# A soft mixture of experts behind sliding-window attention: the expert sum in two PSUM banks, seven filling matmuls, and the output in eleven tiles

## The chip, the cores and the metric

The kernel runs on one core of a Trainium2 chip. The metric is the time of one execution on the device in microseconds (us), inputs and output in the chip's HBM. The core has five engines, which run side by side and wait for each other by semaphores: TensorE (PE; its weight loads are listed apart as PEld), VectorE (DVE), ScalarE (ACT), GpSimd (POOL) and SyncE (SP). Sixteen DMA engines move data between HBM and SBUF, the memory beside the engines. TensorE writes into PSUM, eight banks of 512 fp32 columns on 128 partitions, and DVE and ACT read from there.

## What is computed

The first part is attention over 8 batches, 8 heads, 576 tokens of 64 values. Each token sees 32 earlier ones, side by side for heads 0 to 3 and every fourth for heads 4 to 7. Its result x (4608 rows of 512) goes through a soft mixture of 8 experts with 4 slots each:

```python
logits = x @ phi                                  # 4608 x 32
d = exp(logits - logits.max(0)); d /= d.sum(0)    # each slot over all rows
slot_input = (d.T @ x).reshape(8, 4, 512)
for e in range(8):
    h = np.maximum(slot_input[e] @ w1[e], 0.0)    # 4 x 1024
    slot_out[e] = h @ w2[e]                       # 4 x 512
c = exp(logits - logits.max(1)); c /= c.sum(1)    # each row over the slots
out = c @ slot_out.reshape(32, 512)               # 4608 x 512, fp32
```

## The kernel before

The kernel is written with a tile framework, which puts the instructions in order on each engine, finds the semaphore waits and may move an instruction ahead where nothing holds it back. Only GpSimd's order is as written. GpSimd issues all big loads: q, k and v of the eight batches, and the weights, which are cast from fp32 to fp16 on the way. Each batch and later each expert has one of eight homes in SBUF, so that the weights of expert e can be loaded when batch e is done.

Attention takes most of the time. `unit` goes through four head pairs of each batch, and the front of the expert part is worked into the same loop. `front_logits` (line 430) writes ET, the exponentials of the logits, with 32 slots on 128 partitions (each slot stands four times) and one column for each of the 4608 rows. `front_rows` (line 460) multiplies blocks of 128 columns of ET by `quarter` (0.25), which gives the sum over the slots for 128 rows, and writes the reciprocals to `rrow`, one column for each block of 128 rows.

The expert part starts when the inputs of the slots, siT, are ready. `expert_in` (line 662) does two experts: 32 matmuls with w1 (line 667), a Relu on ACT (line 675), four transposes (line 678) and two copies by DVE into hTp (line 683). `expert_out` (line 688) does eight matmuls of 512 columns with w2. Each takes 32 columns of the array, four of them side by side, and all add into one bank `sop`: 32 slots on four groups of partitions, whose sum is taken later because ET stands four times. The loop calls them for four pairs; the last lines are `expert_out(6)` and `expert_out(7)`. The w2 of expert 7 comes in two halves (lines 250 and 251), chunks 0 to 3 and 4 to 7. ACT then casts `sop` to `so` in fp16 (line 708).

The output goes in 18 tiles of 256 rows (lines 718 to 741). Each partition of a tile holds two neighbouring rows, so that one partition's piece in HBM is 4 KB. For each of the two, one matmul of 512 columns (line 729) multiplies 128 columns of ET (every second one) by `so`. ACT takes the first and DVE the second out of PSUM, each multiplied by its column of `rrow` (lines 731 and 733), into one of six buffers `ot`. SyncE issues one transfer for each tile (line 739). The first tile is made in halves of 256 columns and issued in two transfers (line 737), one for each of the two rows.

Of the kernel before, what the change touches and what calls it, by code (L numbers as in the profile page):

```python
# [9 lines left out]
FP32 = mybir.dt.float32  # L10
# [7 lines left out]
S = 576  # L18
# [6 lines left out]
N_ROWS = B * S  # L25
DMODEL = H * D
E_EXP = 8
# [7 lines left out]
RD, ND = 12, 48  # L35
CL = S // DIL
DW = CL + 16
NU = 4 * B
NV = 2

# [14 lines left out]
def kernel(  # L55
# [10 lines left out]
    nc = tc.nc  # L66
# [5 lines left out]
    ident = consts.tile([128, 128], FP16, name="ident")  # L72
# [4 lines left out]
        out=q0,  # L77
        in_=q[0, 0:2].rearrange("h s d -> (h s) d").rearrange("(g p r) d -> p g (r d)", g=2, r=RP),
# [7 lines left out]
    def kept(shape, name, dt=FP16):  # L86
        return keep.tile(shape, dt, name=name, tag=name)

    ET = kept([128, N_ROWS + 64], "ET")
    csum = kept([128, 2 * B - 2], "csum", FP32)  # L90
    rrow = kept([128, 2 * N_ROWS // 256], "rrow", FP32)
    quarter = kept([128, 1], "quarter")
# [37 lines left out]
    for i in range(NV):  # L130
        nc.vector.memset(vp[i][:, :, :, D : D + 1], 1.0)

    hTp = [kept([128, 8, 60], f"hTp{e}") for e in range(4)]
# [10 lines left out]
    ring = ctx.enter_context(  # L144
        tc.tile_pool(name="ring", bufs=2, space=bass.MemoryType.PSUM)
    )
# [3 lines left out]
    raws, w_tiles = {}, {}  # L150
# [108 lines left out]
    def transposes(u):  # L259
        b, hp = unit(u)  # L260
        for nm in ("q", "k"):
            if nm == "q":
                dst = qT_pool.tile([128, S], FP16, name=f"qT{u}", tag="qT")
                qTs[u] = dst
            else:
                dst = kTp if hp < 2 else kTd
                kTs[u] = dst
            if hp < 2:
                raw = raws[b][nm + "p"]
                rg = ring.tile([128, RP, NP], FP16, name=f"rg{nm}{u}", tag="ring")  # L270
                for r in range(RP):
                    for h in range(2):
                        nc.tensor.transpose(  # L273
                            rg[64 * h : 64 * h + 64, r, :],
                            raw[:, 2 * hp + h, D * r : D * r + D],
                            ident[0:NP, 0:NP],
                        )
                nc.scalar.copy(  # L278
                    out=dst[:, 0:S].rearrange("c (p r) -> c p r", r=RP),
                    in_=rg.rearrange("c r p -> c p r"),  # L280
                )
            else:
                raw = raws[b][nm + "d"]
                rg = ring.tile([128, 3, 4, ND], FP16, name=f"rg{nm}{u}", tag="ring")
                for a in range(3):
                    for cc in range(2):
                        j = 2 * a + cc
                        nc.tensor.transpose(  # L288
                            rg[:, a, 2 * cc : 2 * cc + 2, :].rearrange("c h p -> c (h p)"),
                            raw[:, hp - 2, 128 * j : 128 * j + 128],  # L290
                            ident[0:NP, 0:NP],
                        )
                (nc.scalar.copy if nm == "q" else nc.vector.tensor_copy)(  # L293
                    out=dst[:, 0:S].rearrange("c (g p a) -> c g p a", g=4, a=3),
                    in_=rg.rearrange("c a g p -> c g p a"),
                )

    def scores(u):
# [3 lines left out]
        for part in range(2):  # L302
# [4 lines left out]
            else:  # L307
                todo = [(DW * cc, CL * (2 * cc + part), CL * (2 * cc + part), CL) for cc in range(2)]
                todo += [(DW * cc + CL, None, CL * (2 * cc + part) + 128, 16) for cc in range(2)]
            for at, k0, q0, n in todo:  # L310
                for g in range(2):
                    ks = q0 - 32 * g - 64 * (at // DW) if k0 is None else k0
                    nc.tensor.matmul(  # L313
# [9 lines left out]
    def softmax_parts(u, tiles):  # L323
        b, hp = unit(u)
        for part in range(2):
# [14 lines left out]
            if part == 0:  # L340
                pr = dil_pool.tile([128, 2, 2, 2, DW], FP16, name=f"pd{u}", tag="pd")
            nc.scalar.activation(  # L342
                out=pr[:, part].rearrange("p c e t -> p e c t"),
                in_=st[:, :, 0 : 2 * DW].rearrange("p e (c t) -> p e c t", c=2),
                func=AF.Exp,
                scale=SCALE,
            )
        if hp < 2:
# [10 lines left out]
            out=P2.rearrange("p a c s t -> p (a c) s t")[:, :, :, 0:16],  # L359
            in0=pr[:, :, :, 128:DW].rearrange("p a c (s t) -> p (a c) s t", s=2),  # L360
            in1=mask[:, QW + 64 :].rearrange("p (c s t) -> p c s t", c=8, s=2),
# [90 lines left out]
    def rows(to, tokens, rhs, start, stop):  # L452
        for n, (part, at, step) in enumerate(row_blocks):
            w = step * (part.stop - part.start - 1) + 1
            nc.tensor.matmul(
                to[part, min(n, 9), :], tokens(at, at + w, step), rhs, start=start, stop=stop,
                skip_group_check=True,
            )

    def front_rows(b):  # L460
        r0 = b * S
        t0, t1 = r0 // 256, (r0 + S) // 256
        ep = ring.tile([128, 11, N_SLOTS], FP32, name=f"e{b}", tag="ring")
        if b < B - 1:
            rows(ep, lambda a, z, s: ET[:, r0 + a : r0 + z : s], ident[:, 0:N_SLOTS], True, True)
            nc.vector.tensor_copy(out=Er[b % 2], in_=ep[:, 0:10])
        for n in range(2 * (t1 - t0)):
            c0 = 256 * t0 + 256 * (n // 2) + n % 2
            nc.tensor.matmul(
                ep[:, 10, n : n + 1], ET[:, c0 : c0 + 255 : 2], quarter, start=True, stop=True  # L470
            )
        nc.vector.reciprocal(out=rrow[:, 2 * t0 : 2 * t1], in_=ep[:, 10, 0 : 2 * (t1 - t0)])

    def front_slots(b):
        up = ring.tile([128, DMODEL], FP32, name=f"u{b}", tag="ring")
# [126 lines left out]
    transposes(2)  # L602
    for u in range(NU + 5):
        if u + 1 < NU:
            st = scores(u + 1)
        if u < NU:
            values(u)
        if u + 1 < NU:
            softmax_parts(u + 1, st)
        if u + 3 < NU:  # L610
            transposes(u + 3)
# [11 lines left out]
        if u == 1:  # L623
            spread_phi()
        if u == NU:
            last = ps_s.tile([128, 2, 512], FP32, name="last", tag="s")
# [20 lines left out]
        out=siT,  # L647
# [9 lines left out]
    ps_h = tc.alloc_tile_pool(name="ps_h", bufs=2, space=bass.MemoryType.PSUM)  # L657
    ps_t = tc.alloc_tile_pool(name="ps_t", bufs=2, space=bass.MemoryType.PSUM)
    ps_so = tc.alloc_tile_pool(name="ps_so", bufs=1, space=bass.MemoryType.PSUM)
    sop = ps_so.tile([128, DMODEL], FP32, name="sop", tag="sop")  # L660

    def expert_in(pr):
        hp_ = ps_h.tile([128, 512], FP32, name=f"h{pr}", tag="h")
# [21 lines left out]
                in_=tp[:, :, 2 * ee : 2 * ee + 2, 4 * e : 4 * e + 4].rearrange("p i f s -> p f i s"),  # L685
            )

    def expert_out(e):
        for ch in range(8):
            j = ch % 4  # L690
            nc.tensor.matmul(
                sop[32 * j : 32 * j + 32, :],
                hTp[e % 4][:, ch, 28 - 4 * e : 60 - 4 * e],
                w_tiles[e][1][:, ch, :],
                start=(e == 0 and ch < 4),
                stop=(e == E_EXP - 1 and ch >= 4),
                skip_group_check=True,
            )

    for pr in range(4):  # L700
        expert_in(pr)
# [1 line left out]
            expert_out(2 * pr - 2)  # L703
            expert_out(2 * pr - 1)
    expert_out(6)
    expert_out(7)
    so = keep.tile([128, DMODEL], FP16, name="so", tag="so")
    nc.scalar.copy(out=so, in_=sop)
    ps_so.release()
    ps_t.release()  # L710
    ps_h.release()
# [2 lines left out]

    ps_f = tc.alloc_tile_pool(name="ps_f", bufs=3, space=bass.MemoryType.PSUM)
    out_pool = ctx.enter_context(tc.tile_pool(name="outp", bufs=1))
    ots = [out_pool.tile([128, 2, DMODEL], FP32, name=f"ot{i}", tag=f"out{i}") for i in range(6)]
    for t in range(N_ROWS // 256):
        ot = ots[t % 6]
        rows = out[256 * t : 256 * t + 256, :].rearrange("(m j) d -> m j d", j=2)  # L720
        for j in range(2):
            cols = ET[:, 256 * t + j : 256 * t + j + 255 : 2]
            scale = rrow[:, 2 * t + j : 2 * t + j + 1]
            halves = ((0, 256), (256, 512)) if t == 0 else ((0, 512),)
            for n, (d0, d1) in enumerate(halves):
                n = j if t else n
                fp = ps_f.tile([128, DMODEL], FP32, name=f"f{t}_{j}{n}", tag=f"f{n}")
                fp = fp[:, 0 : d1 - d0]
                nc.tensor.matmul(fp, cols, so[:, d0:d1], start=True, stop=True)  # L729
                if n == 0:  # L730
                    nc.scalar.activation(out=ot[:, j, d0:d1], in_=fp, func=AF.Copy, scale=scale)  # L731
                else:
                    nc.vector.tensor_scalar(  # L733
                        out=ot[:, j, d0:d1], in0=fp, scalar1=scale, scalar2=None, op0=ALU.mult
                    )
            if t == 0:
                nc.sync.dma_start(out=rows[:, j], in_=ot[:, j])
        if t > 0:
            nc.sync.dma_start(
                out=rows.rearrange("m j d -> m (j d)"), in_=ot.rearrange("m j d -> m (j d)")  # L740
            )
    ps_f.release()

# [29 lines left out]
```

## Time and profile before

| what | value |
|---|---|
| median of 3 runs | 185.99 us (185.93 to 188.54) |
| profiled execution | 186.0 us |
| its span, first to last instruction | 184.2 us |
| TensorE busy, DVE busy, ACT busy | 80%, 64%, 63% of the span |
| weights and inputs by GpSimd's queue | 30.79 MB in 22480 packets, 94.4% of the DMA engines' span |
| transfers of SyncE's queue, mostly the output | 9.89 MB in 3376 packets, 13.6% |

The span is counted from the first to the last instruction; what lies before and after it makes the difference to the execution's own time. In the profile's groups, `out<-in` names what an instruction writes and reads, with numbers of buffers left out, and L729 is line 729. A chain of waits is followed back from the last instruction, at each step to what released it. The granted clock is the share of TensorE's full speed that the chip allowed. Ends of matmuls are modelled, so a busy TensorE need not be at its peak.

### The profile page before, as it was taken

What the parts mean: (1) busy time and instruction counts of PE and PEld (TensorE: products, weight loads), DVE (VectorE), ACT (ScalarE), POOL (GpSimd) and SP (SyncE); (2) the same over time, 40 slices, a digit from 0 to 9 for tenths busy, and PEclk for the clock granted to TensorE, in tenths of its full rate; (3) what the DMA queues carried; (4) which work ended last, traced back from release to release, by engine and by line L of the source; (5) the groups of instructions that cost most, each with busy time, mean ns of one, the idle gap of its engine ahead of it and who ended that gap; (6) DMA issues with size and microseconds to landing.
All of it is one profiled execution on the core that took longest, in us unless ns stands there. A gap on an engine that the chain in (4) does not pass through costs nothing.

```text
span 184.2 us, 6078 instructions
## 1 busy us (share of the span) xinstructions
PE 147.0 (80%) x2595; PEld 101.0 (55%) x2595; DVE 117.1 (64%) x363; ACT 116.5 (63%) x208; POOL 48.3 (26%) x77
## 2 busy tenths in 40 slices
PE   1879889699899899979978989989698983895300
PEld 1647666566676667757666667667585330331000
DVE  7605995948778788797786877869801110595610
ACT  2248879677888797798789698878131220785510
POOL 7754545455554545410011010022000000000000
PEclk9999999979999999999999999999965798589755
DMA  5999999999999999999999999999999994399995
GB/s 106 190 202 204 200 202 203 202 201 204 200 203 200 204 201 206 215 211 221 205 223 210 222 206 218 213 216 221 210 222 213 209 212 87 128 422 418 421 418 245
DMA packets 25883, 41.06 MB, mean 223 GB/s; under 512 B 1792, under 2 KB 20352, under 8 KB 24832
## 3 DMA queue, kind: packets, MB, share of 16 engines
q0 software_dynamic: 22480, 30.79, 94.4%
q1 hardware_dynamic: 3376, 9.89, 13.6%
q8 instruction: 20, 0.33, 0.6%
q14 instruction: 7, 0.06, 0.1%
HBM read 62.02 MB, written 9.44 MB: 388 GB/s over the span
## 4 chain that ended last, share of the span: by engine, by line
DMA 54%; PE 15%; issue 14%; ACT 5%; DVE 4%; POOL 4%; ACTq 0%; POOLq 0%
DMA home<-in_moe_w_dram 32%; DMA home<-in_q_dram 6%; DMA home<-in_k_dram 6%; DMA out_dram<-ot 5%; DMA home<-in_v_dram 5%; PE f L729 3%; PE l L434 2%; ACT pd L342 2%; PE sel L203 2%; PE rgx L414 1%; PE o L393 1%; PE rgq L273 1%; POOL home L182 1%; DVE P L351 1%; ACT qT L278 1%
## 5 line engine op out<-in xcount | busy, mean ns | idle before, releaser
L398 DVE TENSOR_TENSOR x<-o,rc 128x384 f16<-128x384 f32 x64 | 30.0, 482 | 0.5
L330 ACT ACTIVATE pr<-s 128x960 f16<-128x960 f32 (+1 forms) x32 | 24.8, 783 | 0.8 <-PE s L313 0.8
L342 ACT ACTIVATE pd<-s 128x640 f16<-128x640 f32 x32 | 21.0, 706 | 0.8 <-PE s L313 0.7
L160 POOL DMA_DIRECT2D home<-in_v_dram x24 | 16.6, 692 | 16.3 <-DMA home<-in_k_dram 9.6
L733 DVE TENSOR_SCALAR ot<-f,rrow 128x512 f32<-128x512 f32 (+1 forms) x19 | 13.3, 720 | 11.1 <-PE f L729 7.3
L203 PE MATMUL sel<-home,pick 32*128 32x256 f16 x128 | 16.8, 291 | 1.2 <-DMA home<-in_v_dram 0.7
L414 PE MATMUL rgx<-ident,x 128*128 128x128 f16 x160 | 14.6, 223 | 3.8 <-ACT qT L293 3.5
L333 DVE TENSOR_TENSOR Pp<-pr,mask 128x960 f16<-128x960 f16 (+2 forms) x48 | 16.4, 394 | 0.3 <-ACT pr L330 0.3
L731 ACT ACTIVATE ot<-f,rrow 128x512 f32<-128x512 f32 (+1 forms) x19 | 12.3, 665 | 6.8 <-DMA out_dram<-ot 4.3
L397 DVE RECIPROCAL rc<-o 128x6 f32<-128x6 f32 x64 | 10.0, 175 | 9.8 <-PE o L393 9.6
L278 ACT COPY qT<-rgq 128x576 f16<-128x576 f16 x16 | 10.3, 642 | 9.3 <-PE rgq L273 8.8
L420 ACT COPY xT<-rgx 128x512 f16<-128x512 f16 x16 | 9.7, 605 | 9.7 <-PE rgx L414 9.7
L729 PE MATMUL f<-so,ET 128*128 128x512 f16 (+1 forms) x38 | 12.3, 454 | 4.4 <-ACT ot L731 3.4
L237 POOL DMA_DIRECT2D home<-in_moe_w_dram x8 | 4.5, 565 | 37.6 <-PE rgq L288 30.1
L211 ACT CAST vp<-sel 128x512 f16<-128x512 f32 x16 | 9.4, 590 | 7.7 <-PE sel L203 7.0
L414 PEld LDWEIGHTS <-x 128*128 128x128 f16 x160 | 9.8, 98 | 7.4 <-issue 5.3
L273 PEld LDWEIGHTS <-home 96*64 96x64 f16 x384 | 11.1, 116 | 4.3 <-issue 2.4
L434 PE MATMUL l<-xT,phi 128*128 128x288 f16 x64 | 11.4, 318 | 2.2 <-ACT qT L278 2.0
L182 POOL DMA_DIRECT2D home<-in_k_dram x16 | 10.6, 662 | 9.4 <-DMA home<-in_q_dram 7.9
L293 DVE COPY kTd<-rgk 128x576 f16<-128x576 f16 x16 | 12.0, 751 | 0.4 <-PE rgk L288 0.4
L393 PE MATMUL o<-vp,Pp 128*128 128x65 f16 x288 | 12.0, 197 | 0.0
L293 ACT COPY qT<-rgq 128x576 f16<-128x576 f16 x16 | 10.4, 647 | 2.2 <-PE rgq L288 1.7
(106 smaller groups left out, 286.6 us busy)
## 6 DMA issues: line engine op xcount, KB each, us to landing
home<-in_moe_w_dram POOLq DMA_DIRECT2D x15, 1024.0 KB, 32.6
out_dram<-ot SPq DMA_DIRECT2D x17, 512.0 KB, 5.0
home<-in_k_dram POOLq DMA_DIRECT2D x16, 288.0 KB, 10.0
home<-in_q_dram POOLq DMA_DIRECT2D x15, 288.0 KB, 9.9
home<-in_v_dram POOLq DMA_DIRECT2D x16, 256.0 KB, 10.0
home<-in_moe_w_dram POOLq DMA_DIRECT2D x2, 512.0 KB, 30.3
home<-in_v_dram POOLq DMA_DIRECT2D x8, 64.0 KB, 8.8
out_dram<-ot SPq DMA_DIRECT2D x2, 256.0 KB, 2.1
```

Source lines behind the costliest of these rows:

```text
L160: nc.gpsimd.dma_start(out=dst, in_=v[b, h0 : h0 + n_h, r0 : r0 + 4 * n_p, :].rearrange("h (p r) d -> p h (r d)", r=4),)
L203: nc.tensor.matmul(sel[:, n, 0], pick[rows, r].rearrange("p i j -> p (i j)"), raw[rows, :, r, :], start=(r == 0), stop=(r == 3), tile_posi ...
L293: (nc.scalar.copy if nm == "q" else nc.vector.tensor_copy)(out=dst[:, 0:S].rearrange("c (g p a) -> c g p a", g=4, a=3), in_=rg.rearrange(" ...
L330: nc.scalar.activation(out=pr, in_=st[:, :, 0:n], func=AF.Exp, scale=SCALE)
L333: nc.vector.tensor_tensor(out=Pp[:, :, b0 : b0 + nb, 0:w], in0=pr[:, :, at : at + nb * w].rearrange("p h (t c) -> p h t c", c=w), in1=mask ...
L342: nc.scalar.activation(out=pr[:, part].rearrange("p c e t -> p e c t"), in_=st[:, :, 0 : 2 * DW].rearrange("p e (c t) -> p e c t", c=2), f ...
L393: nc.tensor.matmul(to, lhs, rhs, start=(n == 0), stop=(n == len(mms) - 1), skip_group_check=True)
L398: nc.vector.tensor_tensor(out=x[:, blocks[0] : blocks[0] + nb, D * hl : D * hl + 2 * D].rearrange("p t (h d) -> p t h d", h=2), in0=ot[:, ...
L414: nc.tensor.transpose(rg[:, 128 * blk : 128 * blk + 128], x[:, blk, hl : hl + 128], ident)
L434: nc.tensor.matmul(lp, phi4[:, kc].rearrange("p a s -> p (a s)"), xT[:, kc, 288 * c : 288 * c + 288], start=(kc == 0), stop=(kc == 3),)
L729: nc.tensor.matmul(fp, cols, so[:, d0:d1], start=True, stop=True)
L733: nc.vector.tensor_scalar(out=ot[:, j, d0:d1], in0=fp, scalar1=scale, scalar2=None, op0=ALU.mult)
```

## The change

Three things change. The expert sum `sop` becomes two banks, of which the first 256 columns of each are used: `expert_out` goes twice over the chunks, with 256 columns of w2 each time, and the cast to `so` is written as one copy by ACT and one by DVE. Between the two halves of expert 7 stand seven matmuls of 512 columns, whose result, `idle`, nobody reads. The output goes in eleven tiles: two of 256 rows, seven of 512 and two of 256, with four buffers of 1 MB in place of six of 0.5 MB. In the larger tiles a partition holds four neighbouring rows, 8 KB in HBM. `front_rows` follows: the columns of ET for each sum are taken with the step of their tile, and a batch makes the reciprocals of all tiles that end in it.

```diff
+OUT_TILES = [(0, 2), (256, 2)] + [(512 + 512 * i, 4) for i in range(7)] + [(4096, 2), (4352, 2)]
+OUT_COLS = [sum(nj for _, nj in OUT_TILES[:i]) for i in range(len(OUT_TILES))]
...
     def front_rows(b):
         r0 = b * S
-        t0, t1 = r0 // 256, (r0 + S) // 256
+        cols = [
+            (n0 + j, t0 + j, nj)
+            for n0, (t0, nj) in zip(OUT_COLS, OUT_TILES)
+            if r0 < t0 + 128 * nj <= r0 + S
+            for j in range(nj)
+        ]
...
-        for n in range(2 * (t1 - t0)):
-            c0 = 256 * t0 + 256 * (n // 2) + n % 2
+        for n, (_, c0, nj) in enumerate(cols):
             nc.tensor.matmul(
-                ep[:, 10, n : n + 1], ET[:, c0 : c0 + 255 : 2], quarter, start=True, stop=True
-            )
-        nc.vector.reciprocal(out=rrow[:, 2 * t0 : 2 * t1], in_=ep[:, 10, 0 : 2 * (t1 - t0)])
+                ep[:, 10, n : n + 1], ET[:, c0 : c0 + 127 * nj + 1 : nj], quarter, start=True, stop=True
+            )
+        if cols:
+            n0 = cols[0][0]
+            nc.vector.reciprocal(out=rrow[:, n0 : n0 + len(cols)], in_=ep[:, 10, 0 : len(cols)])
...
-    sop = ps_so.tile([128, DMODEL], FP32, name="sop", tag="sop")
+    sop = ps_so.tile([128, 2, 512], FP32, name="sop", tag="sop")
...
-    def expert_out(e):
-        for ch in range(8):
-            j = ch % 4
-            nc.tensor.matmul(
-                sop[32 * j : 32 * j + 32, :],
-                hTp[e % 4][:, ch, 28 - 4 * e : 60 - 4 * e],
-                w_tiles[e][1][:, ch, :],
...
+    def expert_out(e, chunks=range(8)):
+        for n in range(2):
+            for ch in chunks:
+                j = ch % 4
+                nc.tensor.matmul(
+                    sop[32 * j : 32 * j + 32, n, 0:256],
+                    hTp[e % 4][:, ch, 28 - 4 * e : 60 - 4 * e],
+                    w_tiles[e][1][:, ch, 256 * n : 256 * n + 256],
...
     expert_out(6)
-    expert_out(7)
+    expert_out(7, range(4))
+    idle = ring.tile([128, 512], FP32, name="idle", tag="ring")
+    for i in range(7):
+        nc.tensor.matmul(idle, ident, ET[:, 512 * i : 512 * i + 512], start=True, stop=True)
+    expert_out(7, range(4, 8))
     so = keep.tile([128, DMODEL], FP16, name="so", tag="so")
-    nc.scalar.copy(out=so, in_=sop)
+    nc.scalar.copy(out=so[:, 0:256], in_=sop[:, 0, 0:256])
+    nc.vector.tensor_copy(out=so[:, 256:512], in_=sop[:, 1, 0:256])
...
-    ots = [out_pool.tile([128, 2, DMODEL], FP32, name=f"ot{i}", tag=f"out{i}") for i in range(6)]
-    for t in range(N_ROWS // 256):
-        ot = ots[t % 6]
-        rows = out[256 * t : 256 * t + 256, :].rearrange("(m j) d -> m j d", j=2)
-        for j in range(2):
-            cols = ET[:, 256 * t + j : 256 * t + j + 255 : 2]
+    ots = [out_pool.tile([128, 4, DMODEL], FP32, name=f"ot{i}", tag=f"out{i}") for i in range(4)]
+    for i, (t0, nj) in enumerate(OUT_TILES):
+        ot = ots[i % 4]
+        rows_out = out[t0 : t0 + 128 * nj, :].rearrange("(m j) d -> m j d", j=nj)
+        halves = ((0, 256), (256, 512)) if i == 0 else ((0, 512),)
+        for j in range(nj):
+            c0, scale = t0 + j, rrow[:, OUT_COLS[i] + j : OUT_COLS[i] + j + 1]
...
-                n = j if t else n
+                n = n if i == 0 else j % 2
...
-        if t > 0:
+            if i == 0:
+                nc.sync.dma_start(out=rows_out[:, j], in_=ot[:, j])
+        if i > 0:
             nc.sync.dma_start(
-                out=rows.rearrange("m j d -> m (j d)"), in_=ot.rearrange("m j d -> m (j d)")
+                out=rows_out.rearrange("m j d -> m (j d)"), in_=ot[:, 0:nj].rearrange("m j d -> m (j d)")
             )
```

More of the change, by code (lines that the diff above doesn't have):

```diff
@@ L686, in expert_in @@
             )
-    def expert_out(e):
-        for ch in range(8):
-            j = ch % 4
-            nc.tensor.matmul(
-                sop[32 * j : 32 * j + 32, :],
-                hTp[e % 4][:, ch, 28 - 4 * e : 60 - 4 * e],
-                w_tiles[e][1][:, ch, :],
-                start=(e == 0 and ch < 4),
-                stop=(e == E_EXP - 1 and ch >= 4),
-                skip_group_check=True,
-            )
+    def expert_out(e, chunks=range(8)):
[6 more added lines that the diff above has]
+                    w_tiles[e][1][:, ch, 256 * n : 256 * n + 256],
+                    start=(e == 0 and ch < 4),
+                    stop=(e == E_EXP - 1 and ch >= 4),
+                    skip_group_check=True,
+                )
     for pr in range(4):
@@ L716 @@
     out_pool = ctx.enter_context(tc.tile_pool(name="outp", bufs=1))
-    ots = [out_pool.tile([128, 2, DMODEL], FP32, name=f"ot{i}", tag=f"out{i}") for i in range(6)]
-    for t in range(N_ROWS // 256):
-        ot = ots[t % 6]
-        rows = out[256 * t : 256 * t + 256, :].rearrange("(m j) d -> m j d", j=2)
-        for j in range(2):
-            cols = ET[:, 256 * t + j : 256 * t + j + 255 : 2]
-            scale = rrow[:, 2 * t + j : 2 * t + j + 1]
-            halves = ((0, 256), (256, 512)) if t == 0 else ((0, 512),)
-            for n, (d0, d1) in enumerate(halves):
-                n = j if t else n
-                fp = ps_f.tile([128, DMODEL], FP32, name=f"f{t}_{j}{n}", tag=f"f{n}")
-                fp = fp[:, 0 : d1 - d0]
-                nc.tensor.matmul(fp, cols, so[:, d0:d1], start=True, stop=True)
+    ots = [out_pool.tile([128, 4, DMODEL], FP32, name=f"ot{i}", tag=f"out{i}") for i in range(4)]
[5 more added lines that the diff above has]
+            c0, scale = t0 + j, rrow[:, OUT_COLS[i] + j : OUT_COLS[i] + j + 1]
+            for n, (d0, d1) in enumerate(halves):
+                n = n if i == 0 else j % 2
+                fp = ps_f.tile([128, DMODEL], FP32, name=f"f{i}_{j}{n}", tag=f"f{n}")[:, 0 : d1 - d0]
+                nc.tensor.matmul(
+                    fp, ET[:, c0 : c0 + 127 * nj + 1 : nj], so[:, d0:d1], start=True, stop=True
+                )
                 if n == 0:
@@ L735 @@
                     )
-            if t == 0:
-                nc.sync.dma_start(out=rows[:, j], in_=ot[:, j])
-        if t > 0:
+            if i == 0:
+                nc.sync.dma_start(out=rows_out[:, j], in_=ot[:, j])
+        if i > 0:
             nc.sync.dma_start(
-                out=rows.rearrange("m j d -> m (j d)"), in_=ot.rearrange("m j d -> m (j d)")
+                out=rows_out.rearrange("m j d -> m (j d)"), in_=ot[:, 0:nj].rearrange("m j d -> m (j d)")
             )
```

## The prediction

> **What bounds the kernel now.** I read the page's row of slices first, then the chain that ended last for 150 to 185 us, then the windows and the timeline around the hand-over. The transfers bound it, in two stages. Up to 156.14 us the weights are read; from 159.6 us the output is written. The chain between the two:
>
> ```profile
> 124.88 31.26 DMA home<-in_moe_w_dram
> 156.14 0.04 issue
> 156.19 0.64 PE sop L691 x4
> 156.83 0.02 issue
> 156.85 0.59 ACT so L708
> 157.44 0.04 issue
> 157.49 6.02 PE f L729 x18
> ```
>
> The last half of w2 lands at 156.14. Four matmuls, one cast and the first output matmul follow one another; nothing lies beside them. The timeline then gives the issues of the output (SPq is SyncE's queue) and the windows the rate at which they flow:
>
> ```profile
> 158.72 0.81 SPq L737 DMA_DIRECT2D out_dram<-ot  x2
> 160.21 18.66 SPq L739 DMA_DIRECT2D out_dram<-ot  x17
> ...
> 159.60:160.80 1.20, 1.20 (x4) 0.41 (x3) 1.10 (x2) 0.87 (x3) 0.00 (x0) 0.50 1.04 401
> 160.80:161.05 0.25, 0.25 (x2) 0.15 (x1) 0.19 (x1) 0.25 (x1) 0.00 (x0) 0.50 0.37 131
> 161.05:171.70 10.65, 7.60 (x27) 2.57 (x25) 7.89 (x11) 6.89 (x11) 0.00 (x0) 0.94 1.03 420
> 171.70:182.30 10.60, 1.13 (x3) 0.10 (x1) 3.01 (x4) 2.75 (x4) 0.00 (x0) 0.54 1.02 417
> ```
>
> After the window come its length, the busy times of PE, PEld, DVE, ACT and POOL, the granted clock, the DMA share and GB/s. The first bytes flow at 159.57, 0.85 us after the first issue. Two transfers of 0.262 MB last to 160.85. The next, issued at 160.21, flows from 161.06, so 0.2 us are lost. From there 8.913 MB go at 418.5 GB/s without a gap: 21.30 us, to 182.36, and the trace ends its bytes at 182.35. From then to the end of the span (184.2) are 1.85 us; the execution took 186.0, 1.8 more. The median of the runs shown, 185.99, is the same time. The end therefore moves only with the moment from which the output flows without a gap, and with its rate.
>
> **The clock.** Windows of 0.1 us put its steps at 145.28 (to 1.00), 155.52 (to 0.50), 162.35 and 172.59. The distances, 10.24, 6.83 and 10.24, are 3, 2 and 3 times 3.41, so I cut the trace into stretches of 3.41 (here the columns end after PE: clock, DMA share, GB/s):
>
> ```profile
> 152.11:155.52 3.41, 0.91 (x15) 1.00 0.55 111
> 155.52:158.93 3.41, 2.06 (x10) 0.50 0.00 0
> 158.93:162.35 3.42, 3.42 (x9) 0.50 0.79 315
> 162.35:165.76 3.41, 3.23 (x13) 1.00 1.03 422
> 165.76:169.17 3.41, 1.88 (x7) 1.00 1.02 418
> 169.17:172.59 3.42, 1.43 (x6) 1.00 1.02 418
> ```
>
> After 0.91 and 1.43 us of PE work the clock falls at the stretch's end; after 1.88 it stays. So a busy time between 1.43 and 1.88 decides. [...]
>
> **The change part by part.** Times are those of the profile before, handed on step by step.
>
> Loads: POOL's list of instructions is the same, so I leave the landing at 156.14.
>
> Row sums: the matmuls by `quarter` change from 6 to 4 for batch 3 and from 6 to 8 for the last batch. These two, and the first of the seven filling matmuls, which the changed program's list puts ahead of the experts' first matmul (it waits for nothing), delay the experts by 0.07 + 0.43 = 0.5 us. PE is idle for 1.10 us before the first half of the last w2 lands (153.7), which hides it. Without that cover it costs 0.5.
>
> Sum in two banks: 64 matmuls of 512 columns become 128 of 256. They stream at 54 ns now (nine in 0.81, the last lasting 0.376: 0.434 / 8). The nearest row for the new form is u, line 481, also 256 columns on 32 columns of the array: ten in 0.51, one lasting 0.273, so 27 ns. At 27 the experts take what they took. If the new form kept 54, it would cost 3 us (a rival below).
>
> Fillers: six stand behind the first half of expert 7. Eight sums of 27 ns from 153.71 end at 153.93; six matmuls of 512 columns at 0.215 (pairs in the trace: two in 0.59, one 0.376) end at 155.22, drained at 155.4. The half of w2 lands 0.8 us later: no cost at clock 1.00. At 0.50 they take 0.427 each and end at 156.65, which costs 0.46. With them the stretch to 155.52 holds about 2.2 to 2.7 us of PE work, above 1.88, so I take the clock as held.
>
> Last sums: four at the low clock took 0.62 to 156.81. Eight at 27 ns and 0.273 take 0.46: 156.65, a gain of 0.16.
>
> Casts: the instruction list of the changed program makes DVE's copy wait for the count that ACT's cast raises, so the two run one after the other. ACT casts 512 columns in 0.586 and exponentiates 320 to 16 bits in 0.438: 256 columns, about 0.38. DVE casts 512 in 0.684 and 320 in 0.481: 256, 0.41. With hand-overs of 0.04 to 0.05 the first output matmul starts at 156.65 + 0.04 + 0.38 + 0.05 + 0.41 + 0.05 = 157.58, not 157.49: it loses 0.25 of the gain. Behind DVE's waiting copy stand only its output evictions, which need the copy anyhow.
>
> First output tile: with the clock at 1.00 the first 256 columns take 0.273, not 0.40, and the second follow after 0.107, not 0.213. ACT starts at 157.88 (0.474), DVE at 158.02 (0.474, done 158.49), and SyncE issues 0.08 later, at 158.57; before, 158.72. Second half: 158.98. Tile 1: PE no longer paces (0.43 each before), DVE does, at 0.676 an eviction in a row (five in 3.38): done 159.66, issue 159.74; before, 160.21.
>
> Tile 2 is now 1.049 MB and needs two evictions on each engine. DVE's end at 161.0; issue 161.06. Flow: 158.57 + 0.85 = 159.42; 0.524 MB at 401 GB/s to 160.73; tile 1 could flow from 160.59, so there is no gap; its 0.524 MB last to 161.98; tile 2 could flow from 161.91. It just fits. At 418.5 the rest ends at 160.73 + 21.30 = 182.03: 0.32 earlier than 182.35. Later tiles come every 1.35 us of DVE against 2.5 us of transfer. With four buffers three transfers of 1 MB stand ahead of each eviction, so the ring does not starve.
>
> Longer rows: 7.34 MB now go in rows of 8 KB. Rows of 2 KB ran at 401 GB/s, of 4 KB at 418.5. If a fixed time per row explains this, 8 KB gives 428, which is 0.4 us in 17.5; the other bounds are nothing (rows may be cut in pieces of 4 KB) and a loss of 0.77, the 401 of the smallest row, since no row of the trace shows a store of this size. I take 0.2: the row of 4 KB is the nearest and speaks for nothing, the line through both rows for 0.4, and I stand half way. [...]
>
> Sum: 186.0 - 0.32 - 0.2 = **185.5 us**.
>
> **Rivals.** *The clock is not held* (slower). Place: the stretch that ends before the last sums. If its PE work stays under the deciding 1.43 to 1.88, the eight sums take 0.77 (0.053 apart, then 0.40), the casts 0.93, and output starts at 157.89, 0.40 later than before. Tile 2 now needs what tiles 2 and 3 needed, whose issue came at about 161.92: 162.32, flow at 163.17, 8.389 MB at 418.5 to 183.2, so +0.87, less 0.2 for rows: 186.7. If the fillers ran at 0.50 too, 187.1. For it: a stretch that began at 152.9 would hold only some 1.8 us. Against it: at the boundaries of this trace it holds 2.2 or more. [...]
>
> *Sums at 54 ns*: 7 x 0.43 + 0.5 - 1.08 = 2.4 us late at the first half, 1.7 at the second, and 0.2 more in the last eight: 187.4. Row u speaks against it.
>
> *Rows of 8 KB are slower*: 185.7 + 0.77 = 186.5. *The casts do overlap*, so that the split does what its words say: 0.4 less before the first output, 185.1; the waits in the list speak against it.
>
> **How the numbers follow.** Forecast 0.60 (185.2 to 185.9 by its bounds); clock not held 0.17; rows slower 0.07; sums at 54 ns 0.06; overlapping casts 0.05; other things 0.05, half of them slower. From 184.9 to 187.0 lie the forecast, the overlap, the slower rows and most of the clock's case, about 0.85; what is above is left out. Both signs are in it; the forecast's own range is given. 2% (3.7 us) is about what a measurement can tell from no change. No rival reaches it alone, so within 2% gets 0.95, slower 0.03 (two rivals together), faster 0.02.
>
> **What would show it.** Held clock: granted clock 1.00 from 153 to 158.9, four filling matmuls per 0.86 us, PE idle before the last sums. Casts: DVE's starts after ACT's ends, first f at about 157.6. Tiles: issues at about 158.6, 159.0, 159.7, 161.1 and no dip in GB/s after. Rows: 418 to 430 GB/s from then on. Wrong would be: a landing of w2 away from 156.1, PE still in fillers when it lands, or a gap in the flow before tile 2.

## The result, and the profile after

The changed kernel takes 187.24 us (median of 22 runs) against 186.18 (22 runs of the kernel before). The ratio is 1.0051, with a 95% interval of 1.0031 to 1.0070: slower by about 0.95 us, where 0.5 us less was forecast. That is inside what 2% can tell from no change, but it lies above the forecast's range and on the other side. Some runs of all kernels are longer by several us; the ratios here and below, and the medians given with the experiments, leave those out.

The profiled execution took 187.18 us, its span is 185.4. First the page's rows that answer to the ones before: the slices, the clock, the DMA queues.

```profile
PE   1879888699899989979978989989799986874400
...
PEclk9999999879999999999999999999955899997555
...
q1 hardware_dynamic: 2368, 9.89, 13.2%
q8 instruction: 21, 0.34, 0.7%
```

The same rows of the kernel before, for the clock and for q8:

```profile
PEclk9999999979999999999999999999965798589755
...
q8 instruction: 20, 0.33, 0.6%
```

TensorE's low stretch behind the experts is gone, as forecast: the clock is up from 145.2 to 169.1 us. The output needs 1008 fewer packets. One thing is new that I had not looked for: queue q8, which brings instructions, has 21 packets in place of 20.

Then the chain of waits from the landing of the weights to the first output:

```profile
125.51 31.36 DMA home<-in_moe_w_dram
156.88 0.04 issue
156.92 0.42 PE sop L700 x8
157.35 0.02 issue
157.37 0.38 ACT so L721
157.75 0.02 issue
157.78 0.44 DVE so L722
158.21 0.04 issue
158.25 0.28 PE f L741
```

The weights land at 156.88, later than the 156.14 of before. The last sums take 0.42 us in place of 0.64, the two casts run one behind the other (0.38 and 0.44), and the first output matmul starts 1.33 us behind the first of the last sums; before, 1.30. SyncE issues the first transfer at 159.23, 2.31 us behind it (before 2.53).

Last, the windows over the flow of the output, of the kernel after. The columns are length, busy time of PE, PEld, DVE, ACT and POOL, clock, DMA share and GB/s.

```profile
161.00:182.00 21.00, 8.36 (x25) 2.82 (x24) 10.20 (x15) 8.78 (x15) 0.00 (x0) 0.69 1.02 425
182.00:182.60 0.60, 0.00 (x0) 0.00 (x0) 0.00 (x0) 0.00 (x0) 0.00 (x0) 0.50 0.49 198
182.60:183.00 0.40, 0.00 (x0) 0.00 (x0) 0.00 (x0) 0.00 (x0) 0.00 (x0) 0.50 0.05 20
183.00:184.00 1.00, 0.00 (x0) 0.00 (x0) 0.00 (x0) 0.00 (x0) 0.00 (x0) 0.50 0.06 25
184.00:184.80 0.80, 0.00 (x0) 0.00 (x0) 0.00 (x0) 0.00 (x0) 0.00 (x0) 0.50 0.01 5
```

And the same windows of the kernel before:

```profile
161.00:182.00 21.00, 8.79 (x29) 2.67 (x27) 10.90 (x15) 9.69 (x15) 0.00 (x0) 0.74 1.02 419
182.00:182.60 0.60, 0.00 (x0) 0.00 (x0) 0.00 (x0) 0.00 (x0) 0.00 (x0) 0.50 0.51 205
182.60:183.00 0.40, 0.00 (x0) 0.00 (x0) 0.00 (x0) 0.00 (x0) 0.00 (x0) 0.50 0.03 10
183.00:184.00 1.00, 0.00 (x0) 0.00 (x0) 0.00 (x0) 0.00 (x0) 0.00 (x0) 0.50 0.00 0
```

Here is where the time went. In both kernels the bulk of the bytes is out at about 182.3 us, although the changed kernel began its output 0.5 us later: it writes faster (425 against 419 GB/s). But behind that it goes on at 20 to 25 GB/s until 184.2. A share of 0.05 to 0.06 is one engine of sixteen (1/16 is 0.0625). One DMA engine is 1.9 us behind the others, and the kernel ends when it does. I call this stretch, from the moment at which the first engines run dry to the last byte, the tail. Before, it was 0.6 us (the expectations below count from a little later and say 0.5).

What can hold one engine? The DMA queues of the changed kernel in the window from 165 to 175 us (packets, MB, share of 16 engines):

```profile
q1 hardware_dynamic: 597, 4.26, 101.4%
q8 instruction: 1, 0.02, 0.6%
```

The kernel before, in the same window, has only this row:

```profile
q1 hardware_dynamic: 1152, 4.19, 102.6%
```

One packet of 16 KB of instructions, at 165.6 us, and 0.6% of 16 engines over 10 us is 0.96 us of one engine. The kernel before has no q8 packet behind 152.5 us. TensorE's matmuls went from 2595 to 2666, each with a weight load, so 142 instructions more; 2595 pairs took 20 packets, one for some 260 instructions. The change makes TensorE's program just long enough for a twenty-first, and it falls into the output.

### The profile page after: what moved, and what is told of

Read it like the earlier page. It is cut to its first block, busy times and chain, and to the rows that moved or that the text cites. A ratio compares the mean times of both kernels' runs of the same rounds, so it can differ in the third digit from the quotient of the medians.

```text
span 185.4 us, 6196 instructions
## 1 busy us (share of the span) xinstructions
PE 147.4 (80%) x2666; PEld 104.0 (56%) x2666; DVE 117.1 (63%) x364; ACT 115.0 (62%) x208; POOL 48.3 (26%) x77
## 4 chain that ended last, share of the span: by engine, by line
DMA 55%; issue 14%; PE 12%; DVE 6%; ACT 5%; POOL 3%; POOLq 0%; ACTq 0%; DVEq 0%; SPq 0%
DMA home<-in_moe_w_dram 32%; DMA out_dram<-ot 8%; DMA home<-in_v_dram 6%; DMA home<-in_k_dram 6%; DMA home<-in_q_dram 4%; PE l L436 2%; ACT pd L344 2%; PE sel L205 2%; ACT ot L745 2%; DVE P L353 1%; DVE x L400 1%; PE rgx L416 1%; PE o L395 1%; PE rgq L275 1%; DVE ot L747 1%
## 5 line engine op out<-in xcount | busy, mean ns | idle before, releaser
L747 DVE TENSOR_SCALAR ot<-f,rrow 128x512 f32<-128x512 f32 (+1 forms) x19 | 12.5, 717 | 7.3 <-DMA out_dram<-ot 6.8
L745 ACT ACTIVATE ot<-f,rrow 128x512 f32<-128x512 f32 (+1 forms) x19 | 11.2, 675 | 9.0 <-DMA out_dram<-ot 8.1
L280 ACT COPY qT<-rgq 128x576 f16<-128x576 f16 x16 | 10.3, 642 | 10.1 <-PE rgq L275 9.6
L741 PE MATMUL f<-so,ET 128*128 128x512 f16 (+1 forms) x38 | 11.1, 404 | 5.7 <-ACT ot L745 4.6
L395 PE MATMUL o<-vd,P 128*128 128x65 f16 (+1 forms) x256 | 10.2, 196 | 2.3 <-DVE P L353 2.3
```

What stands on the lines that cost most here:

```text
L395: nc.tensor.matmul(to, lhs, rhs, start=(n == 0), stop=(n == len(mms) - 1), skip_group_check=True)
L747: nc.vector.tensor_scalar(out=ot[:, j, d0:d1], in0=fp, scalar1=scale, scalar2=None, op0=ALU.mult)
```

## Experiments

Two theories for the tail were set against each other: the fetch of instructions, and the rows of 8 KB, which might let the engines drift apart. Four kernels tell them apart, two by taking parts of the change alone, two by changing nothing but the number of TensorE's instructions.

### The eleven tiles alone

The sum, the cast and expert 7 are as before; `OUT_TILES`, `front_rows` and the output loop are those of the changed kernel. The diff is against the changed kernel.

```diff
-    sop = ps_so.tile([128, 2, 512], FP32, name="sop", tag="sop")
+    sop = ps_so.tile([128, DMODEL], FP32, name="sop", tag="sop")
...
-    expert_out(7, range(4))
...
-    expert_out(7, range(4, 8))
+    expert_out(7)
...
+    nc.scalar.copy(out=so, in_=sop)
```

> The kernel before with nothing but the eleven output tiles (sum in one bank, one cast, no fillers). In the changed kernel the sixteen DMA engines stop at 182.4 us but for one, which goes on to 184.2; before, the last one stops 0.5 us after the others. Fetch theory: the tail comes from a fetch of 16 KB of TensorE's instructions (queue q8, 0.96 us on one engine) that falls into the output in the changed kernel, because it has 142 more TensorE instructions. Then this kernel has no q8 packet after the first issue, a tail of about 0.5 us, and a time of 186.0 to 186.4, the clock being low (tile 2 is late by 0.5 us, the long rows give 0.5 back). Row theory: rows of 8 KB let the engines drift apart, whatever is fetched. Then the tail is 1.5 to 2 us here too, and the time about 187.3.

Measured: 186.25 us, ratio 0.9982 (0.9952 to 1.0011). There is no q8 packet in the output, and the tail is 0.1 us: the bulk ends at 182.9 us, the last byte comes at 183.0. So the long rows do not make the tail. The first windows show a gap in the flow ahead of tile 2 (0.73 of the engines' time from 162 to 163), since that tile needs four matmuls of 0.43 us at half clock and is issued only at 162.37; the last two show the end:

```profile
160.00:161.00 1.00, 1.00 (x4) 0.42 (x3) 0.90 (x2) 0.79 (x2) 0.00 (x0) 0.50 1.03 397
161.00:162.00 1.00, 1.00 (x6) 0.39 (x4) 0.90 (x2) 0.88 (x2) 0.00 (x0) 0.80 0.88 352
162.00:163.00 1.00, 1.00 (x5) 0.45 (x4) 1.00 (x3) 1.00 (x3) 0.00 (x0) 1.00 0.73 299
163.00:164.00 1.00, 1.00 (x5) 0.45 (x4) 1.00 (x2) 1.00 (x3) 0.00 (x0) 1.00 0.93 393
...
182.60:183.00 0.40, 0.00 (x0) 0.00 (x0) 0.00 (x0) 0.00 (x0) 0.00 (x0) 0.50 0.72 287
183.00:184.00 1.00, 0.00 (x0) 0.00 (x0) 0.00 (x0) 0.00 (x0) 0.00 (x0) 0.50 0.00 0
```

### The sum and the fillers alone

The changed kernel with the output tiles of before.

```diff
-OUT_TILES = [(0, 2), (256, 2)] + [(512 + 512 * i, 4) for i in range(7)] + [(4096, 2), (4352, 2)]
+OUT_TILES = [(256 * i, 2) for i in range(18)]
...
-    ots = [out_pool.tile([128, 4, DMODEL], FP32, name=f"ot{i}", tag=f"out{i}") for i in range(4)]
+    ots = [out_pool.tile([128, 2, DMODEL], FP32, name=f"ot{i}", tag=f"out{i}") for i in range(6)]
...
-        ot = ots[i % 4]
+        ot = ots[i % 6]
```

> The changed kernel with the output of before (eighteen tiles of 256 rows, rows of 4 KB, six buffers), so sum in two banks, two casts and fillers alone. Fetch theory: the TensorE instructions are as many as in the changed kernel, so one q8 packet falls into the output, the tail is 1.5 us or more, and with 4 KB rows, 0.5 us slower, the time is 187.2 to 187.6. Row theory: tail 0.5 us, time 185.8 to 186.3.

Measured: 187.46 us, ratio 1.0084 (1.0051 to 1.0118). There is a q8 packet at 166.5, and a tail of 1.8 us (183.5 to 185.24), with rows of 4 KB:

```profile
183.00:184.00 1.00, 0.00 (x0) 0.00 (x0) 0.00 (x0) 0.00 (x0) 0.00 (x0) 0.50 0.57 229
184.00:184.80 0.80, 0.00 (x0) 0.00 (x0) 0.00 (x0) 0.00 (x0) 0.00 (x0) 0.50 0.06 26
```

This profile also caught the rival of the clock. First TensorE's timeline, then two windows (the clock is the third number from the end):

```profile
154.57 0.40 PE L700 MATMUL sop<-home,hTp 128*32 128x256 f16 x8 [2.09 <-DMA home<-in_moe_w_dram]
154.91 2.74 PE L718 MATMUL idle<-ET,ident 128*128 128x512 f16 x6
157.58 0.62 PE L700 MATMUL sop<-home,hTp 128*32 128x256 f16 x8
```

```profile
154.00:155.00 1.00, 0.43 (x9) 0.21 (x9) 0.00 (x0) 0.00 (x0) 0.00 (x0) 0.94 0.57 115
155.00:156.00 1.00, 1.00 (x3) 0.34 (x4) 0.00 (x0) 0.00 (x0) 0.00 (x0) 0.50 0.25 49
```

The experts were done early here, TensorE stood idle for 2.09 us, and its clock fell just as the fillers began. They took 2.74 us in place of 1.47, and the last sums, whose weights had landed at about 156.7, began at 157.58 (no wait is shown ahead of them): in this trace about 0.9 us are lost to the fillers themselves.

### As many instructions, nothing else

The kernel before, with 71 matmuls of one column behind the warm-up, where TensorE waits for its first data.

```diff
     warm(6, ring, "ring")
+    tiny = ring.tile([128, 512], FP32, name="tiny", tag="ring")
+    for _ in range(71):
+        nc.tensor.matmul(tiny[:, 0:1], ident, ident[:, 0:1], start=True, stop=True)
```

> The kernel before with 71 more matmuls of one column behind the warm-up, where TensorE waits for its first data anyway: as many TensorE instructions as the changed kernel, nothing else touched. Fetch theory: one more q8 packet, in the output, tail 1.5 us, time up by about 1.0 to 187.1. Row theory, and any theory that looks to the edits themselves: no change, 186.1.

Measured: 187.55 us, ratio 1.0070 (1.0051 to 1.0089), 0.45 us more than expected. The page counts 21 q8 packets, with nothing added but matmuls: q8 carries TensorE's instructions. The last one comes at 167.2, in the output, and the last windows show a tail of 1.9 us:

```profile
182.60:183.00 0.40, 0.00 (x0) 0.00 (x0) 0.00 (x0) 0.00 (x0) 0.00 (x0) 0.50 0.56 225
183.00:184.00 1.00, 0.00 (x0) 0.00 (x0) 0.00 (x0) 0.00 (x0) 0.00 (x0) 0.50 0.08 33
184.00:184.80 0.80, 0.00 (x0) 0.00 (x0) 0.00 (x0) 0.00 (x0) 0.00 (x0) 0.50 0.05 20
```

Small matmuls at the very start made the kernel 1.3 us slower, and the tail, at the very end, is 1.3 us longer than before. (In this one trace the output also begins 0.5 us later, at 160.07, behind weights that land later.) No edit of the output is needed for that.

### Still more instructions, to move the fetch out of the way

The changed kernel with `range(32)` in the same place.

> The changed kernel with 32 more matmuls of one column behind the warm-up. The last q8 fetch comes at 165.7 us some 64 instructions behind the start of the last sums, so 64 more instructions ahead move it to about 157, where no data flow. Fetch theory: more instructions make it faster, by about 1.0 us, to 186.1, tail 0.5 us. Row theory: no change, 187.1.

Measured: 185.49 us, where 186.1 was expected; ratio 0.9965 to the kernel before (0.9948 to 0.9981). Against the changed kernel that is 0.9965 / 1.0051 = 0.9914, or 1.6 us, won by adding instructions. In the trace the experts begin eight us late, so it can't be laid beside the changed kernel's; a second trace can:

> The changed kernel with 32 more matmuls of one column, once more, for a trace in which the experts are not late: the last fetch at about 157 us or in the wait before it, no q8 packet behind the first issue, and the last engine at most 0.8 us behind the others.

This trace (185.6 us) is a twin of the changed kernel's. The weights land at 156.83 (156.88 there), the first output matmul starts at 158.21 (158.25), the first transfer is issued at 159.18 (159.23). Its q8 packet came at 156.0, with no transfer of the output about, and its windows end thus:

```profile
161.00:182.00 21.00, 7.66 (x25) 2.65 (x24) 10.16 (x15) 8.74 (x15) 0.00 (x0) 0.74 1.02 427
182.00:182.60 0.60, 0.00 (x0) 0.00 (x0) 0.00 (x0) 0.00 (x0) 0.00 (x0) 0.50 0.38 150
182.60:183.00 0.40, 0.00 (x0) 0.00 (x0) 0.00 (x0) 0.00 (x0) 0.00 (x0) 0.50 0.00 0
```

The tail is 0.2 us, and the span is 183.8 against 185.4. Up to the end of the bulk the two traces agree within 0.1 us; what differs is the tail. With the 71 small matmuls, which brought the tail into the kernel before, this settles the cause.

### A whole fetch more

If fetches load one engine, they might pace the loads as well. The kernel before with `range(128)` has 256 TensorE instructions more, about one packet's worth by the some 260 above, and no q8 packet in the output.

> The kernel before with 128 more matmuls of one column behind the warm-up: 256 instructions more, one whole fetch, so that all later fetches come as in the kernel before and none lands in the output. If a fetch costs only when it hits the end of the output, nothing changes: 186.2. If the loads too are paced by the one engine that also carries the fetches, the last weights land up to 0.95 us later and the time is 186.7 to 187.2.

Measured: 186.6 us, ratio 1.0015 (0.9984 to 1.0045); the last packet of the weights was in at 155.9 us, in the kernel before at 155.8. The 0.95 us (0.5%) lie just outside the interval, so that many instructions more at the start cost less than that, and nothing was seen at the landing. It is also the control for the 71: 128 small matmuls in the same place, but no fetch in the output, and no 0.7%. In this trace it was TensorE that was late: the experts began at 145.8 us, not at 140.7.

### The casts

The changed kernel, with no instructions added; only the tile of two banks is cut in two tiles, and `expert_out` writes to `sops[n]`.

```diff
-    sop = ps_so.tile([128, 2, 512], FP32, name="sop", tag="sop")
+    sops = [ps_so.tile([128, 512], FP32, name=f"sop{n}", tag=f"sop{n}") for n in range(2)]
...
-    nc.scalar.copy(out=so[:, 0:256], in_=sop[:, 0, 0:256])
-    nc.vector.tensor_copy(out=so[:, 256:512], in_=sop[:, 1, 0:256])
+    nc.scalar.copy(out=so[:, 0:256], in_=sops[0][:, 0:256])
+    nc.vector.tensor_copy(out=so[:, 256:512], in_=sops[1][:, 0:256])
```

> The changed kernel with the sum in two tiles of one bank each in place of one tile of two banks, and nothing else: the two casts then wait for TensorE alone and not for each other. By the serial theory the wait of DVE's cast for ACT's cost 0.4 us, so the first output matmul starts 0.4 us earlier behind the landing of w2 (0.95 in place of 1.35 us). The last fetch stays in the output, so the tail stays at 2 us and the time is about 186.7. If the two casts hinder each other at PSUM, each takes longer than the 0.37 and 0.42 of the changed kernel.

In the timeline of this kernel the casts overlap, each as long as before, and the first output matmul starts 0.93 us behind the last sums (158.12 to 159.05) in place of 1.33:

```profile
158.46 0.37 ACT L721 CAST so<-sop 128x256 f16<-128x256 f32 x1 [3.45 <-PE sop L700]
158.57 0.42 DVE L722 CAST so<-sop 128x256 f16<-128x256 f32 x1 [2.80 <-PE sop L700]
```

So the wait cost 0.40 us, and it came from the framework's order of two readers of one PSUM tile. The one run took 188.03 us, where 186.7 was expected. The fetch is there (q8 at 166.5, tail 1.9 us), as expected; the rest has another reason. The chain of waits:

```profile
157.97 0.22 PE idle L718
158.19 0.36 PE sop L700 x8
```

The experts began at 145.0 us, the fillers at 156.72, when the last packet of the weights had been in since 155.8. So the fillers stood in the way by their whole length, 1.4 us.

### The fillers, and kernels with both mends

> The changed kernel without its seven filling matmuls, and with 39 matmuls of one column behind the warm-up, so that the last fetch of instructions lands where it does in the kernel with 32 more. Against that one (0.9965 of before), only the fillers are missing. If the fillers hold the clock, this one is slower by 0.5 to 0.9 us (last sums at half clock, first output late, tile 2 waits for matmuls of 0.43): 186.1 to 186.5. If the fillers are often themselves too late for the clock, and then stand in the way of the last sums, as in the profile with small tiles, the two are equal within 0.3 us.

Without the fillers, and with 39 small matmuls to keep the fetch in its place: 0.9984 of before (0.9957 to 1.0012), against 0.9965 with them. The difference of 0.35 us is within both intervals, so no gain from the fillers is shown.

> The eleven tiles and the seven fillers with the sum in one bank and one cast by ACT, as before: 128 fewer TensorE instructions than the changed kernel, so no fetch lands in the output. Fetch theory: tail 0.5 us. The one cast (0.59) stands against two in a row (0.37 + 0.42 and a hand-over), so it is also 0.2 us faster up to the first output matmul: 185.3 to 185.6. If the sum in two banks had a merit of its own, this kernel would be slower than the one with 32 more matmuls (0.9965 of before).

One bank, one cast, eleven tiles and the fillers, so no fetch in the output: 0.9989 (0.9958 to 1.0020). Its trace has a tail of 0.2 us and a span of 183.8, with the last packet of the weights at 156.6. But the runs spread from 184.75 to 186.96. The median, 186.54, is 0.9 to 1.2 us more than was expected; why is open, and so is whether the sum in two banks has a merit of its own.

> The changed kernel with both mends: the sum in two tiles of one bank, so that the casts overlap, and 32 matmuls of one column behind the warm-up, so that the last fetch falls between the stages. Fetch theory and serial theory together: tail 0.5 us, first output matmul 0.95 us behind the start of the last sums, 0.4 us less than with 32 more alone (0.9965 of before): 0.994 of before, 185.1.

> The same without the seven filling matmuls, and with 39 in place of 32 of one column, so that the fetches stay where they are. In the traces so far TensorE reached the last half of w2 anywhere from 3 us before its landing to 2 us behind it, since the first loads start the attention early or late. If the fillers' gain in the early runs (clock held: about 0.7 us) outweighs their cost in the late ones (up to 1.3 us on the path), this kernel is slower than the one with fillers by 0.3 us; if the late ones weigh as much, the two are equal, 0.994 to 0.996 of before.

With overlapping casts and the fetch moved: 0.9989 (0.9957 to 1.0021) with fillers, 0.9962 (0.9933 to 0.9990) without. Both traces have a tail of 0.2 us. The 0.4 us that the casts save can be seen in the trace, but not in these times. In the trace with fillers the experts' last chunk was done only at 157.8 and the fillers ran to 159.15, 2.4 us behind the last packet of the weights. So the expected 0.994 was missed. In one pair of kernels the one with fillers is the faster, in the other the one without, both times within the intervals: over many runs no worth of the fillers is shown. The kernels at 0.9962 and 0.9965 are the two whose intervals lie below the kernel before, by a third of a per cent; they cannot be told from each other.

## Why the prediction was wrong

**The step that failed** is the one that closed the first part: "The end therefore moves only with the moment from which the output flows without a gap, and with its rate." It carried the 1.85 us from the last bulk byte to the end of the span over as a constant. In them lies the tail, which belongs to the slowest of sixteen engines, and it grew by 1.3 us (1.9 in place of 0.6): from the end of the bulk, 182.3, to the end of the span, 185.4, are now 3.1 us. Behind it stands a term that the sum lacked. The part on two banks counted 64 matmuls more, and the part on fillers seven more, as time on TensorE alone. They are also bytes: 142 instructions with their weight loads, and one packet of 16 KB more, through the same DMA engines that bound the kernel. The page of before had the row that could have told it, q8 with 20 packets, and 2595 pairs of instructions to divide by it. With this term (+1.3) the sum would have been 186.8, against 187.18 in the profile. That it comes so near is in part luck. Of the 1.7 us between 185.5 and 187.18 only some 1.25 lie behind the bulk; 0.45 lie ahead of it, for the bulk ended at 182.3 and not at the forecast's 181.8 (182.03 less 0.2), behind weights that landed 0.74 us later than forecast.

In the trace of before, q8's 20 packets of 16 KB take 0.89 to 1.09 us each. The cost of one more fell on the transfers: behind 1.0070 for the kernel with nothing but 71 small matmuls more stands a fetch in the output.

The other steps, one by one:

- *Clock held.* Right in this profile: no low clock from 145.2 to 169.1. The rival was right in another: with small tiles the clock fell at 154.9 and the fillers took 2.74 us. Both happen. The deciding 1.43 to 1.88 us of PE work fit two more traces from the hand-over on (in the changed kernel the clock stayed at 158.85 behind 1.77 and fell at 169.09 behind 1.39; without fillers it fell at 157.4 behind 1.54), but they are no rule for the whole kernel: in the trace of before the clock fell at 135.0 behind a stretch of 3.41 us, from 131.62, that holds 2.95 us of PE work.
- *Fillers cost nothing.* Wrong as a rule. The forecast took one trace's arrival of TensorE (idle 1.10 us before the first half, 2.07 before the second) as fixed. In most of the traces here the experts begin between 140.0 and 146 us, in two still later, while the last packet of the weights comes between 155.8 and 156.8 whatever the start. When TensorE came late, the fillers were on the path, with 1.4 us in the kernel with two tiles for the sum.
- *Sums of 256 columns at 27 ns.* Right: eight in 0.40, a stretch of 17 in 0.72, which is (0.72 - 0.273) / 16 = 28 ns. The rival at 54 ns is out.
- *Casts one behind the other.* Right, with 0.38 and 0.44 against 0.38 and 0.41. That it is the wait that costs 0.4 was shown by the two tiles, in the trace and not in the time.
- *First tiles.* From the start of the last sums to the first issue 2.38 us were forecast, 2.31 came; to tile 1, 3.55 forecast, 3.36 came. The flow had no gap ahead of tile 2.
- *Long rows.* The sign was right, the size too small. I stood half way, at 0.2 us; in the packets' records a row of 8 KB goes as one packet (896 of them) and takes 309 ns against 2 x 159 for two of 4 KB, and the flow reached 425 to 427 GB/s, where the line through both rows had 428: 0.4 us.
- *Landing at 156.14.* It came at 156.88. Nothing in the change was found to do that: the last packet of the weights, 0.33 us ahead of what the chain calls the landing in both, came between 155.8 and 156.8 us in all traces, of kernels with few and with many instructions alike.

Take the fetch away and the time is near the forecast: 0.9965 of 186.0 is 185.35, where 185.5 was said. This too is in part luck. In the trace with the fetch moved (185.6 us) the weights landed 0.7 us later than the forecast took, and a tail shorter than before's (0.2 for 0.6), the long rows (0.2 more than said) and the steps up to the first issue (0.1) made up for it. What the held clock is worth was not shown by the times at all. A mechanism that was not on the list decided.

## What to carry to other kernels

DMA bounds the end of this kernel, and there the instructions were traffic too: one packet of 16 KB, 0.96 us of one engine, came with a tail of 1.9 us in place of 0.6. In a kernel of that kind, count the packets of the instruction queue in the page, divide TensorE's instructions by them, and see whether an edit that adds matmuls pushes another fetch into the last transfers. If so, try to move it: here 32 small matmuls at the start, whose result nobody reads, won 1.6 us. And where the end shows about one sixteenth of the DMA share, here 0.05 to 0.06, look for one engine's tail, and ask what else that engine had to carry.

## What was not expected of the hardware

A fetch of 16 KB took 0.89 to 1.09 us (q8's packets in the traces of before and after; 0.96 for the one in the output), but in the four traces that had one in the output the tail is 1.8 to 1.9 us, in the nine others 0.1 to 0.6, and the engines did not even it out in the some 15 us of flow that were left. Why it is more than 0.96 can be read in part from the packets' own records. They name no engine, but in the output of the changed kernel 99% of the packets of 8 KB start within 4 ns of the end of another, so that they can be chained by their ends and starts, and I take one chain for one engine. In the changed kernel the two packets of 8 KB ahead of the fetch took 0.50 and 0.60 us and the one behind it 0.67, where such a packet otherwise takes 0.31. Beyond the usual time that is 0.84, with the fetch 1.80 us: nearly the whole tail. In the trace with two tiles for the sum they took 0.47, 0.60 and 0.67. What stretches the neighbours is open.

The tail of 0.6 us of the kernel before looks like the same thing in small: one packet of 8 KB of queue q14, which the page also calls instruction, falls into its output at 178.7 us (0.31 us), and the chain in which it lies is the one that ends last. No experiment was made on that.

Open is also what lets the experts begin at 140 us in one run and at 146 in another. The traces show that the whole attention is shifted from its first batch on (the first batch's slot sums start between 44.3 and 49.8 us), but not why, and no experiment was made on it.
